# A sorted-block attention and its feed-forward layer on one core: loads issued ahead of GpSimd's own work, and every engine's list ordered anew

## The chip, the cores and the metric

The kernel runs on one core of a Trainium2 chip. A core has five engines that run side by side, each with its own list of instructions, taken strictly in order: TensorE (PE, matrix products; its loads of weights are shown as PEld), VectorE (DVE), ScalarE (ACT), GpSimd (POOL) and SyncE (SP). They wait for one another on semaphores. Transfers are issued from an engine's list (here from GpSimd and SyncE) and then run by themselves. The metric is device time in microseconds (us); less is better.

## What is computed

Four batches of eight heads, 768 positions, head size 64. Eight blocks of 96 keys and values per head are mixed by an 8x8 matrix P, which five rounds of a Sinkhorn iteration make from `sort_net`; then each block of queries attends to its own mixed block, and the result goes through a feed-forward layer of 2048 with a learned slope for negative values.

```python
P = sort_net                                   # [4, 8, 8, 8]
for _ in range(5):
    P = np.exp(P - max over the last axis)
    P = P / sum over the last axis
    P = P / sum over the axis before it
k_sorted = einsum('bhij,bhjcd->bhicd', P, k in blocks)     # v the same
attn = softmax(q_b @ k_sorted_b.T / 8)                     # per block of 96
x = (attn @ v_sorted_b), heads side by side                # [3072, 512]
h = x @ w_in                                               # [3072, 2048]
out = (max(h, 0) + alpha * min(h, 0)) @ w_out              # [3072, 512], float32
```

## The kernel before

The kernel is written as a graph. Each call of `G.add` names an engine (or a choice of engines), a function that issues the instructions, the keys that it reads and writes, a duration for a plan, and for a transfer its semaphore. There are 1222 such operations, numbered in the order in which they are added. The order in which they run is a table, `SEQ`: a list of these numbers. Each engine's list is the part of the table that belongs to it; a letter after a number (`97a`, `91d`) chooses ScalarE, VectorE or GpSimd where there is a choice.

`arrange` walks through the table and gives each operation a planned start and end, from durations and delays that are written in the code. The plan issues nothing by itself. It is used in two places: `emit` works out from the graph which semaphore waits are needed, and `fill` and `idle` put filling products into TensorE's list where the plan shows it waiting. These (line 1054) multiply the identity by itself into a free accumulator bank. `fill` works from the end of the bfloat16 identity `identb`, 5 us at the earliest, up to the second attention product; in a gap it puts 0.9 times the gap over 0.215 us of them.

The work of the opening, by the lines of the profile. Copies between tiles go through one helper and are all shown at line 429.

- Line 949: `BURST`, 110 products of 32x32 on zeros, at the start of TensorE's list.
- Lines 480, 464, 955, 963: loads from GpSimd, which convert to bfloat16: v and k of batch 0 (`VST`, `KS`), q (four parts), two halves of `w_in`, two of `w_out`. All go through one GpSimd queue.
- Lines 507, 521, 535: GpSimd's memsets. Line 507 clears `VDz`, the tile into which v is copied; for batch 0 in two halves, key `VD0`. Line 512: the select that makes the identity.
- Lines 579 to 593: the Sinkhorn steps on VectorE, with the exponential on ScalarE (582). Their result is `Pb`. Lines 600 and 604 spread it to the mixing matrix `BDK`.
- Line 657: the products that mix k of batch 0 (six steps), copied to `KT`; line 745: the same for v (eight steps), copied to `VS`, from `VDz`, whose eight pieces were copied from `VST` before (`conv_v`, line 723 of the file).
- Lines 782, 788, 794, 803, 826, 835: the attention of a head group (one block of all eight heads of a batch; 32 groups in all): score products, maximum, scores again with the maximum subtracted, exponential, product with v. Groups 0 to 7 take this path. Groups from 8 on use lines 782, 788, 815 (eight exponentials), 820 (a transposing transfer) and 835.
- Lines 884, 894, 897: FFN1, a step of four products, with ScalarE making `t` and VectorE making `hT`. Line 923: FFN2, a step of four products.

For batches 1 to 3, v's copies go into a ring of four slots of `VDz` (`conv_v`, second part), 64 partitions at a time: the lower half on GpSimd, the upper half too, but for batch 1 on ScalarE or VectorE as the table says.

## Time and profile before

| what | us |
|---|---|
| median of three timed runs | 248.17 |
| lowest, highest of them | 247.64, 251.79 |
| the profiled execution, its own time | 245.73 |
| its span in the trace | 243.7 |
| first FFN1 product starts | 28.98 |
| first FFN2 product starts | 40.83 |
| first score product of group 8 starts | 61.31 |

A row of the timeline gives the start, the busy time, the engine, the line and the operation, what it writes and reads (partitions x elements), how many instructions are merged, and in brackets how long the engine stood idle before it and what ended that. A busy TensorE is not TensorE at its peak: products are pipelined and their ends are modelled.

### The profile page before, as it was taken

Reading aid. Unit: us, or ns where it says so; the run is one execution under the profiler, and the core shown is the slowest. Engines: PE = TensorE matmul, PEld = TensorE weight load, DVE = VectorE, ACT = ScalarE, POOL = GpSimd, SP = SyncE. Lnnn points to the kernel's source line nnn. Section 1 sums busy time; section 2 is a strip of 40 time slices with the busy share of each in tenths; the row PEclk is TensorE's granted clock in tenths of the full one; section 3 lists DMA queues with packets and bytes.
Section 4 is the critical chain, followed back from the end, with each engine's and each line's share of the span. In section 5 each row is a group of like instructions: output and inputs, shape, how many; then the busy total and the mean of one; then the engine's idle time right before and its main releaser. Section 6 shows DMA issues by size and latency. Waiting matters only on the chain.

```text
span 243.7 us, 6078 instructions
## 1 busy us (share of the span) xinstructions
PE 224.3 (92%) x2410; PEld 135.5 (56%) x2439; DVE 174.6 (72%) x346; ACT 153.6 (63%) x422; POOL 101.4 (42%) x143
## 2 busy tenths in 40 slices
PE   1099999999877999999999999999999999999995
PEld 1056677886533666665655566555555555555553
DVE  5655589896999997878877787867777766554440
ACT  4327756767777799776885876667745674454331
POOL 7628282739799984528494954100000000000000
PEclk9999999999999999999999999999999999999999
DMA  5998999987999836762999443542453225312113
GB/s 95 197 200 124 190 208 210 172 154 107 215 152 106 76 97 127 168 133 42 172 148 175 119 56 70 120 113 54 90 158 66 52 75 67 102 39 92 42 46 129
DMA packets 65213, 28.99 MB, mean 119 GB/s; under 512 B 56849, under 2 KB 59937, under 8 KB 65185
## 3 DMA queue, kind: packets, MB, share of 16 engines
q0 software_dynamic: 25856, 13.64, 42.0%
q1 hardware_dynamic: 39328, 14.97, 28.8%
q8 instruction: 19, 0.31, 0.5%
q14 instruction: 10, 0.07, 0.1%
HBM read 27.28 MB, written 6.29 MB: 138 GB/s over the span
## 4 chain that ended last, share of the span: by engine, by line
PE 81%; DVE 9%; DMA 3%; ACT 3%; issue 2%; ACTq 0%; POOLq 0%
PE psH L884 30%; PE psYP L923 27%; PE psS L923 4%; PE psS L782 3%; DMA VST<-in_v_dram 3%; PE psO L835 3%; DVE VDz L429 3%; PE psYP L1054 3%; DVE hT L897 2%; PE psYP L699 2%; PE psYP L740 2%; PE psS L794 1%; PE psYP L884 1%; DVE VS L429 1%; PE psO L860 1%
## 5 line engine op out<-in xcount | busy, mean ns | idle before, releaser
L897 DVE SCALAR_TENSOR_TENSOR hT<-t,omaT,psH 128x384 bf16<-128x384 f32 (+1 forms) x131 | 74.9, 580 | 32.8 <-ACT t L894 31.5
L884 PE MATMUL psH<-xT,w_in_bf 128*128 128x384 bf16 (+1 forms) x524 | 95.2, 315 | 1.2 <-DVE hT L897 1.1
L894 ACT ACTIVATE t<-psH 128x384 f32<-128x384 f32 (+1 forms) x131 | 61.1, 470 | 50.4 <-PE psH L884 45.7
L923 PE MATMUL psYP<-w_out_bf,hT 128*128 128x512 bf16 x308 | 78.1, 379 | 1.7 <-issue 0.3
L884 PEld LDWEIGHTS psH<-xT,w_in_bf 128*128 128x128 bf16 x524 | 46.6, 98 | 31.1 <-DVE hT L897 3.4
L815 ACT ACTIVATE Esb<-psS,nf 96x96 bf16<-96x96 f32 x192 | 46.2, 344 | 2.5 <-DVE nf L788 2.4
L923 PEld LDWEIGHTS psYP<-w_out_bf,hT 128*128 128x128 bf16 x336 | 30.6, 98 | 28.8
L429 POOL COPY VDz<-VST 64x384 bf16<-64x384 bf16 (+1 forms) x45 | 38.1, 847 | 14.1 <-DMA VST<-in_v_dram 6.6
L686 POOL COPY KSz<-KS 64x512 bf16<-64x512 bf16 x36 | 22.0, 612 | 22.7 <-PE psYP L699 15.1
L788 DVE TENSOR_REDUCE nf<-psS 96x8 f32<-96x768 f32 x24 | 22.8, 949 | 4.8 <-PE psS L782 4.7
L455 POOL DMA_DIRECT2D QN<-in_q_dram x24 | 19.9, 845 | 9.0 <-PE psO L674 5.4
L845 DVE TENSOR_TENSOR xq<-psO,rec 96x512 bf16<-96x512 f32 x31 | 21.2, 685 | 0.8
L1054 PE MATMUL psYP<-identb 128*128 128x512 bf16 x21 | 7.6, 464 | 9.8 <-ACT identb L429 9.8
L835 PEld LDWEIGHTS psO<-VS,ET 112*128 112x128 bf16 x248 | 11.1, 97 | 3.9 <-ACT xT L429 0.2
L835 PE MATMUL psO<-VS,ET 112*128 112x65 bf16 x248 | 12.7, 194 | 0.0
L782 PE MATMUL psS<-KT,QT 64*96 64x96 bf16 x248 | 11.7, 214 | 0.1
L782 PEld LDWEIGHTS psS<-KT,QT 64*96 64x96 bf16 x248 | 7.9, 120 | 6.9 <-ACT t L894 2.2
L740 PEld LDWEIGHTS psYP<-BDV,VDz 128*128 128x128 bf16 x192 | 7.9, 98 | 6.7 <-DVE VDz L429 2.1
L740 PE MATMUL psYP<-BDV,VDz 128*128 128x64 bf16 x192 | 9.6, 193 | 2.2 <-DVE VDz L429 1.2
L429 ACT ACTIVATE outstg<-psYP 128x512 f32<-128x512 f32 x15 | 9.1, 604 | 3.8 <-PE psYP L923 3.7
L842 DVE RECIPROCAL rec<-psO 96x8 f32<-96x8 f32 x31 | 6.2, 200 | 6.6 <-PE psO L835 6.4
L429 ACT ACTIVATE VS<-psYP 112x512 bf16<-112x512 f32 x14 | 9.6, 686 | 2.0 <-PE psYP L740 1.8
(129 smaller groups left out, 206.9 us busy)
## 6 DMA issues: line engine op xcount, KB each, us to landing
out_dram<-outstg SPq DMA_DIRECT2D x23, 256.0 KB, 2.4
QN<-in_q_dram POOLq DMA_DIRECT2D x26, 96.0 KB, 4.3
KS<-in_k_dram POOLq DMA_DIRECT2D x3, 768.0 KB, 10.7
w_in_bf<-in_moe_w_in_dram POOLq DMA_DIRECT2D x2, 1024.0 KB, 11.6
w_out_bf<-in_moe_w_out_dram POOLq DMA_DIRECT2D x2, 1024.0 KB, 16.0
VST<-in_v_dram POOLq DMA_DIRECT2D x4, 384.0 KB, 6.4
VST<-in_v_dram POOLq DMA_DIRECT2D x1, 768.0 KB, 7.5
VST<-in_v_dram POOLq DMA_DIRECT2D x4, 192.0 KB, 4.5
```

Of the source, the lines that this page charges most:

```text
L429: return e.activation(o, i, ACTF.Copy) if e is nc.scalar else e.tensor_copy(o, i)
L686: G.add(POOL, lambda e, hp=hp: e.tensor_copy(AP(KSz, hp * 64 * 3072 + u % 3 * 1024 + hp * 64, [[3072, 64], [128, 8], [1, 64]]), AP(KS[n], ...
L740: inst = e.matmul(AP(t, off + dd * 64, [[row, 128], [1, 64]]), AP(VDz, (u % VSL * 8 + dd) * 128, [[VSL * 1024, 128], [1, 128]]), AP(BDV, b ...
L782: inst = e.matmul(o, AP(QT[n], hp * 64 * 3072 + h4 * 768 + i * 96, [[3072, 64], [1, 96]]), AP(KT[n], hp * 64 * ld + (i * 4 + h4) * bk, [[l ...
L788: G.add(DVE, lambda e: e.tensor_reduce(AP(nx, 0, [[8, 96], [4, 2], [1, 4]]), AP(psX, 0, [[1024, 96], [512, 2], [96, 4], [1, 96]]), AxisLis ...
L815: inst = e.activation(AP(Esb[me], p * 128, [[1024, 96], [64, 2], [1, 48]]), AP(psX, (p // 4) * 512 + (p % 4) * 96, [[1024, 96], [48, 2], [ ...
L835: inst = e.matmul(AP(psZ, hp * 512 + h4 * 68, [[1024, 128], [1, 65]]), AP(ET[me] if far else ET[m], pos(h4, hp) * 96, [[800, nk], [1, 128] ...
L845: G.add(DVE, lambda e: e.tensor_tensor(out=AP(xq[me], 0, [[512, 96], [256, 2], [64, 4], [1, 64]]), in0=AP(psZ, 0, [[1024, 96], [512, 2], [ ...
L884: inst = e.matmul(AP(pt, poff, [[1024, 128], [1, n]]), AP(w_in_bf, kt * DFF + ft * 128, [[KT_TILES * DFF, 128], [1, 128]]), AP(xT, kt * XR ...
L894: G.add(ACT, lambda e: e.activation(AP(t1[tb], 0, [[384, 128], [1, n]]), AP(pt, poff, [[1024, 128], [1, n]]), ACTF.Relu, scale=-1.0), t_ac ...
L897: G.add(DVE, lambda e: e.scalar_tensor_tensor(out=AP(hT, ft * RING + tok % RING, [[FT_TILES * RING, 128], [1, n]]), in0=AP(t1[tb], 0, [[38 ...
L923: inst = e.matmul(AP(bank[0], bank[1], [[1024, 128], [1, n]]), AP(hT, ft * RING + tok % RING, [[FT_TILES * RING, 128], [1, 128]]), AP(w_ou ...
```

## The change

- `SEQ` is a new order of all operations, and some choices of engine in it differ. One operation is gone (the two memsets of `VD0` are one), so the numbers from 20 on stand for the operation after.
- In GpSimd's list the identity's select comes right after v's load, then k, all four parts of q, both halves of `w_in` and the first half of `w_out`, then the memset of `VD0` and three copies of v. Before, memsets and copies stood between these loads, and the second half of `w_in` and both of `w_out` came after five copies of v.
- Copies of v of batch 0: from five on GpSimd, one on ScalarE, two on VectorE to three, one and four. On ScalarE and VectorE they stand behind the last Sinkhorn step of that engine.
- `identb` is ScalarE's first operation; it was behind the fifth exponential.
- `VD0` clears only the pad columns 48 to 63 of each 64 of `VDz`, in one memset of 128x512 in strips of 8, and not all of it.
- `BURST` is 226.
- Over the whole program ScalarE takes four copies of v of batch 1 (one before) and VectorE four (seven before); 15 copies of KT (12) fall to ScalarE, 11 of xT (7) to VectorE.
- Constants of the plan change: the engines' first free times, the delay after a block of TensorE instructions (6000 to 5500 ns), three durations. `behind` is recorded with an operation; no line shown here reads it.

```diff
-BURST = 110
+BURST = 226
 SEQ = """
-4 18 5 2 3 14 0 15 40 41 42 26 43 44 45 46 27 47 48 49 50 37 19 51 52 53 54 55 30 56 57 58 59 60 61 62 97a 6 7
+2 4 21 14 18 15 17 16 3 0 39 40 41 42 43 44 45 46 47 25 48 49 36 50 51 5 52 53 54 37 55 56 57 58 59 6 7 8 60
...
-    def add(self, eng, fn, dur, r=(), w=(), prio=0.0, dma=None, modes=(0, 0), how="load"):
+    def add(self, eng, fn, dur, r=(), w=(), prio=0.0, dma=None, modes=(0, 0), how="load", behind=()):
         op = _Op(eng, fn, dur, prio, dma, len(self.ops))
-        op.modes, op.how = modes, how
+        op.modes, op.how, op.behind = modes, how, [x.idx for x in behind]
...
-        free = {"pool": 400.0, "sync": 0.0, "pe": 0.0, "act": 1200.0, "dve": 0.0}
+        free = {"pool": 1300.0, "sync": 800.0, "pe": 1040.0, "act": 2050.0, "dve": 870.0}
...
-                    usable = y + (3300 if y < 3000 else 6000 if y < 38000 else 4500 if y < 66000 else 2600)
+                    usable = y + (3300 if y < 3000 else 5500 if y < 38000 else 4500 if y < 66000 else 2600)
...
-        zero_v("VD0", -95.5, [])
+        G.add(POOL, lambda e: e.memset(AP(zv, 24, [[VSL * 512, 128], [32, 64], [1, 8]]), 0.0), 640,
+              w=[("VD0", 0), ("VD0", 1)], prio=-95.5)
...
             G.add(EITHER if b == 1 and th else POOL, lambda e, o2=o2, i2=i2: copy(e, o2, i2),
-                  {"act": 868, "dve": 525, "pool": 835}, r=vst, w=[("VDz", u % VSL, th)], prio=prio)
+                  {"act": 868, "dve": 900, "pool": 845}, r=vst, w=[("VDz", u % VSL, th)], prio=prio)
```

## The prediction

> **What bounds the kernel now.** I read the page first: busy shares, slices, chain.

> ```profile
> PE 224.3 (92%) x2410; PEld 135.5 (56%) x2439; DVE 174.6 (72%) x346; ACT 153.6 (63%) x422; POOL 101.4 (42%) x143
> PE   1099999999877999999999999999999999999995
> PE 81%; DVE 9%; DMA 3%; ACT 3%; issue 2%; ACTq 0%; POOLq 0%
> ```

> TensorE is busy 92% of the span and makes 81% of the chain. The slices show two weak places: the first 12 us, and the slices from about 61 to 79 us. Then I asked for the busy time in stretches and, for the early part, the timeline.

> ```profile
> 18.00:23.00 5.00, 5.00 (x105) 2.96 (x100) 2.91 (x5) 3.79 (x7) 4.11 (x6) 1.00 0.78 107
> 61.31:79.25 17.94, 14.64 (x147) 7.69 (x149) 17.25 (x25) 13.76 (x40) 15.99 (x20) 1.00 1.22 158
> 82.00:240.00 158.00, 156.42 (x1302) 89.74 (x1324) 110.78 (x194) 101.67 (x293) 45.75 (x64) 1.00 0.52 96
> ```

> The columns are length, then busy time of PE, PEld, DVE, ACT, POOL, granted clock, DMA share and GB/s. From 82 us on TensorE misses 1.6 us of 158, so a new order of the lists can gain next to nothing there. From 61.31 to 79.25 it misses 3.3 us while VectorE is busy 17.25 of 17.94: VectorE is the bound of that stretch. So the gain has to come from the opening and from that stretch.

> **The change, part by part.** *Sinkhorn.* The chain of small VectorE and ScalarE steps that ends in Pb:

> ```profile
> 4.83 0.26 ACT L582 ACTIVATE P<-P 32x64 f32<-32x64 f32 x1 [1.31 <-DVE P L593]
> 6.59 0.26 ACT L582 ACTIVATE P<-P 32x64 f32<-32x64 f32 x1 [0.98 <-DVE P L593]
> 8.10 0.21 DVE L593 TENSOR_TENSOR P<-P,cs 32x64 f32<-32x64 f32 x1
> 8.93 0.85 ACT L429 ACTIVATE VDz<-VST 128x384 bf16<-128x384 bf16 x1 [2.09 <-DMA VST<-in_v_dram]
> 9.69 0.24 ACT L582 ACTIVATE P<-P 32x64 f32<-32x64 f32 x1
> 12.95 0.31 DVE L593 TENSOR_TENSOR Pb<-P,cs 32x64 bf16<-32x64 f32 x1
> ```

> An iteration takes 6.59 - 4.83 = 1.76 us. The fourth exponential should start at 6.59 + 1.76 = 8.35 and starts at 9.69, because ScalarE, in order, has a copy of v ahead of it that waits for v to land. The new list puts no copy of v on ScalarE before the fifth exponential, so Pb ends 1.34 us earlier: 13.26 becomes 11.92. The fill of sel0, ahead of the fourth reduction on VectorE, goes to before the first, where VectorE waits for sort_net.

> *From Pb to the first k product.*

> ```profile
> 1.04 1.07 PE L949 MATMUL psS<-bz 32*32 32x32 bf16 x110 [1.04 <-DVE bz L943]
> 11.95 1.89 PE L1054 MATMUL psYP<-identb 128*128 128x512 bf16 x4 [9.84 <-ACT identb L429]
> 13.77 0.38 PE L600 MATMUL psYP<-Pb,sel 32*128 32x8 bf16 x8
> 14.08 1.46 PE L1054 MATMUL psYP<-identb 128*128 128x512 bf16 x3
> 14.19 0.29 DVE L604 TENSOR_TENSOR BDK<-mkh,psYP 128x128 bf16<-128x128 f32 x1 [0.93 <-PE psYP L600]
> 15.94 0.69 PE L657 MATMUL psO<-BDK,KS 64*64 64x64 bf16 x32
> 21.35 1.25 PE L1054 MATMUL psYP<-identb 128*128 128x512 bf16 x5
> ```

> BDK is there at 14.48 and the k products start at 15.94: the filling products before them ran at 1.89/4 = 0.47 us each, at 21.35 the same five took 0.25 each. The filling is counted out in the plan at 0.215. The change makes identb before the first exponential (it was after the fifth), so the filling can run from about 5 us: (11.9 - 5.0) x 0.9 / 0.215 gives some 29 products, 25 if the plan puts the end of the 226 opening products near 5.9. The granted clock says 1.00 in every stretch, so the slow rate shows in durations alone. It lasted from 11.95 to 15.54, 3.6 us; 8 products go slowly, 17 to 21 at 0.215, 7.1 to 8.1 us in all, from 5.3 to 12.4 or 13.4. That overruns Pb by 0.5 to 1.5; before, the product L600 also stood 13.77 - 13.26 = 0.51 behind Pb. I keep 0.51, and BDK ends 1.22 after Pb as before, at 13.1, with TensorE fast; if nothing overruns, at 12.6.

> [...]

> The 226 cost TensorE 226 x 1.07/110 = 2.2 us that it otherwise idles; nothing waits for it before 5 us. A pause within them, bounded by Pb at 11.92, is hidden too.

> *Loads.*

> ```profile
> 2.66 0.29 POOL L512 TENSOR_SCALAR_AFFINE_SELECT identf<-identf 128x128 f32<-128x128 f32 x1
> 3.00 0.95 POOL L507 MEMSET VDz<- 128x1024 f32 x1
> KS<-in_k_dram POOLq DMA_DIRECT2D x1, 768.0 KB, 10.7
> 20.30 0.79 POOL L955 DMA_DIRECT2D w_in_bf<-in_moe_w_in_dram  x1
> 43.89 1.27 POOL L686 COPY KSz<-KS 64x512 bf16<-64x512 bf16 x2 [5.87 <-DMA KS<-in_k_dram]
> ```

> The select now stands before k's issue (0.3 us later, with v's bytes still ahead), after which seven issues follow with no fill between. k, issued at 1.98, lands at 12.7; so it is the next thing late, at 12.7 to 13.0, level with BDK. The second w_in, issued at 20.30 behind copies and fills, goes to about 7 (k's issue and five more ahead of it, at most 0.8 each). The stretch from 18 to 23 us moved 107 GB/s; filling that in ends the later loads about 2.5 us sooner, which GpSimd's 5.87 us wait at 43.89 feels and TensorE, busy there, does not. I cost it at nothing; the cover is that wait being GpSimd's own. One memset of 128x512 in strips replaces two of 128x1024: between 0.3 and 0.95 us, and under the loads either way.

> *The opening after BDK.* The new list gives VectorE, between BDK and the first attention product (L835), four copies of v, three of KT, four of VS, two maxima and six small pieces.

> ```profile
> L429 DVE COPY VDz<-VST 128x384 bf16<-128x384 bf16 x2 | 1.3, 640 | 0.0
> L429 DVE CAST KT<-psH 128x512 bf16<-128x512 f32 x3 | 2.0, 685 | 0.0
> L429 DVE CAST VS<-psO 112x512 bf16<-112x512 f32 x1 | 0.7, 693 | 0.7 <-PE psO L745 0.7
> L788 DVE TENSOR_REDUCE nm<-psS 96x8 bf16<-96x768 f32 x1 | 1.0, 955 | 2.1 <-PE psS L782 2.1
> 14.39 0.38 DVE L540 TENSOR_REDUCE mkjV<-identf 128x8 f32<-128x128 f32 x1
> 25.76 0.30 PEld L835 LDWEIGHTS psO<-VS,ET 112*128 112x128 bf16 x8
> ```

> The copies of v are 0.64 here and 0.99 from 61 to 79 us, where GpSimd copies beside them (next part). GpSimd's copies in the opening are listed first and end about 12, so I take 0.64; by 0.99 it is 1.4 us more and the gain below is 0.6.

> [...]

> The sum is 4 x 0.64 + 3 x 0.69 + 4 x 0.69 + 2 x 0.95 = 9.3, with 1.3 for the six (each at most 0.38) 10.6. From 13.1 this ends at 23.7, against 25.76 now: 2.0 us earlier. Bounds: Pb alone, less an overrun of 1, leaves 0.3; with BDK at 12.6 it is 2.5. Before, VectorE had idle time in this stretch (2.1 us ahead of the first maximum); now it is the bound.

> *The stretch of 61 to 79 us.* It runs from the first score product of head group 8 to its attention product. VectorE made seven copies of v here (the second halves), and ScalarE one; the new list gives four to each.

> ```profile
> L429 DVE COPY VDz<-VST 64x384 bf16<-64x384 bf16 x7 | 6.9, 987 | 0.2
> L894 ACT ACTIVATE t<-psH 128x384 f32<-128x384 f32 x8 | 4.0, 495 | 3.0 <-PE psH L884 3.0
> L429 ACT ACTIVATE VS<-psYP 112x512 bf16<-112x512 f32 x4 | 2.7, 687 | 0.8 <-PE psYP L740 0.8
> L429 ACT ACTIVATE VDz<-VST 64x384 bf16<-64x384 bf16 x1 | 0.9, 872 | 0.0
> 63.02 1.93 ACT L815 ACTIVATE Esb<-psS,nf 96x96 bf16<-96x96 f32 x8 [0.22 <-DVE nf L788]
> 117.25 1.30 PE psH L884 x8
> 121.60 1.73 PE psYP L923 x8
> ```

> VectorE's list there is now 4 maxima, 4 VS, 4 copies of v and 3 hT: 3.8 + 2.8 + 3.9 + 1.8 = 12.3. ScalarE becomes the bound: 3 x 1.93 + 4 x 0.50 + 4 x 0.87 + 4 x 0.69 + one out copy of 0.6 = 14.6, against 17.94: 3.3 us less. But the stretch now holds 4 FFN1 and 7 FFN2 steps where it held 7 and 6; 3 x 0.65 - 0.86 = 1.1 us of products moves to where TensorE is full. The net is 2.2. ScalarE's copies queue ahead of its exponentials; if each of its sixteen pieces waits 0.14, nothing remains; if the moved products fit into holes, 3.3.

> *The rest.* The planner's constants and the recorded `behind` issue no instruction; they reach the chip through the list and the filling counts. From 82 us on: nothing, plus or minus 1.

> **The sum.** 2.0 + 2.2 = 4.2 us off the profiled 245.73 (span 243.7 and 2 us around it): 241.5. The three timed runs have a median of 248.17, 2.4 above that execution; off it, the time is 244.0.

> **The rivals.** *More comes of it (241.5).* BDK ends at 12.6, the moved products fit, and the holes between 29 and 61 us shrink: 0.5 + 1.1 and 0.9 of the idle there:

> ```profile
> 28.00:32.00 4.00, 3.63 (x62) 2.51 (x62) 2.40 (x8) 2.53 (x6) 0.79 (x1) 1.00 1.17 177
> 45.00:60.00 15.00, 14.74 (x212) 11.53 (x213) 11.48 (x29) 11.03 (x27) 10.32 (x19) 1.00 1.13 139
> ```

> For it: k lands early enough, and v and k of the second batch come sooner. Against it: those 0.4 and 0.3 us of idle are mostly waits of one head group's own chain, which the change keeps.

> *ScalarE takes VectorE's place (246.2).* Its copies of v push the exponentials, and the middle gains nothing; 2.0 remains. For it: ScalarE was already 13.76 busy of 17.94. Against it: its list sums to less than the stretch.

> *The filling overruns (slower: 252.7 to 255.9).* If the array stays at the slow rate, 29 products of 0.47 take 13.6 us, from 5.3 to 18.9; L600, BDK and VectorE's 10.6 us follow and L835 comes at 19.6 + 10.6 = 30.2, 4.5 us late; from the plan's 5.9 it is 5.1. With the middle unchanged that gives 252.7 to 253.3, and it decides once more than 17 products run slowly. Against it: the rate changed 3.6 us after the filling began. For it: nothing in the list can skip a filling product. It goes past 254 if ScalarE's three more copies (2.6) also come on top in the middle.

> **How the numbers follow.** The forecast has 0.40, and its own range is 242.5 to 246; two fifths of it lie under 243.2, which is 2% off 248.17 (about what a measurement of this kernel can tell from no change). The rival with more has 0.30, ScalarE 0.12, the overrun 0.18, three fifths of it over 2%. Faster: 0.16 + 0.30 = 0.46; slower: 0.11; the rest, 0.43, within. The range from 240.5 to 250 takes in the first three cases and their bounds, and leaves out most of the overrun.

> **What would show it.** Right: the fourth exponential near 8.35, Pb near 11.9, the k products at 13 and the first L835 near 23.7; then a stretch from the first score product of group 8 to its L835 under 16 us, with ScalarE fuller than VectorE. Wrong: filling products still running when Pb is there by over 1 us, k products waiting for k's load, or a late L835 of group 8 with ScalarE idle.

## The result and the profile after

| what | before | after |
|---|---|---|
| median of four timed runs | 247.9 | 244.66 |
| lowest, highest of them | 247.26, 251.79 | 243.8, 248.17 |
| the profiled execution, its own time | 245.73 | 243.8 |
| its span in the trace | 243.7 | 242.0 |
| first k product | 15.94 | 14.03 |
| first attention product (the prediction's L835) | 25.76 | 26.40 |
| first FFN1 product | 28.98 | 30.22 |
| first score product of group 8 | 61.31 | 63.32 |
| attention product of group 8 | 79.25 | 76.88 |

Time after over time before is 0.9866, with a 95% interval of 0.9819 to 0.9913: the changed kernel is faster, by less than 2%. One execution of each kernel (251.79 and 248.17), over 1.5% longer than the fastest of its own, is left out of this ratio. The forecast was 244.0. That the number fits hides that one half of the sum went the other way: the opening, forecast 2.0 us shorter, became longer, and the rest of the program gained about what was forecast.

In the changed file the lines of the table of before stand one to three further down: L583 is the exponential, L587 and L594 the two-input Sinkhorn steps, L602 the spread of Pb, L606 BDK, L659 the k products, L747 the v products, L784, L790 and L817 the scores, maximum and exponentials, L837 the attention product, L886 and L925 FFN1 and FFN2, L951 the opening products, L1057 the filling.

Page of the kernel after: busy time, slices, granted clock in slices, chain.

```profile
PE 230.2 (95%) x2545; PEld 138.8 (57%) x2574; DVE 172.1 (71%) x350; ACT 152.3 (63%) x420; POOL 98.1 (41%) x140
PE   3997999999999999999999999999999999999995
PEclk9999799999999999999999999999999999999999
PE 83%; ACT 8%; DVE 4%; issue 3%
```

The weak slices at 61 to 79 us are gone, and the first three are fuller, since opening products and filling now stand there. New are a 7 of TensorE's in the fourth slice (18 to 24 us) and a 7 in the row of the granted clock, in the fifth; before, that row held nines only.

Timeline of the kernel after, the opening, all engines:

```profile
1.00 2.02 PE L951 MATMUL psS<-bz 32*32 32x32 bf16 x223 [1.00 <-DVE bz L945]
6.14 0.21 PE L951 MATMUL psS<-bz 32*32 32x32 bf16 x3 [3.12 <-issue]
6.28 6.99 PE L1057 MATMUL psYP<-identb 128*128 128x512 bf16 x24
8.29 0.26 ACT L583 ACTIVATE P<-P 32x64 f32<-32x64 f32 x1 [1.51 <-DVE P L594]
8.95 2.62 POOL L429 COPY VDz<-VST 128x384 bf16<-128x384 bf16 x3 [0.26 <-DMA VST<-in_v_dram]
9.04 0.81 DVE L587 TENSOR_TENSOR P<-P,rs 32x64 f32<-32x64 f32 x1
10.40 0.35 DVE L594 TENSOR_TENSOR P<-P,cs 32x64 f32<-32x64 f32 x1
12.30 0.21 DVE L594 TENSOR_TENSOR Pb<-P,cs 32x64 bf16<-32x64 f32 x1
13.20 0.37 PE L602 MATMUL psYP<-Pb,sel 32*128 32x8 bf16 x8
14.03 0.44 PE L659 MATMUL psH<-BDK,KS 64*64 64x64 bf16 x16
21.99 0.38 PE L747 MATMUL psO<-BDK,VDz 128*64 128x64 bf16 x11 [1.50 <-issue]
22.40 0.69 DVE L429 CAST VS<-psO 112x512 bf16<-112x512 f32 x1 [1.81 <-PE psO L747]
26.40 0.54 PE L837 MATMUL psO<-VS,ET 112*128 112x65 bf16 x8
```

Three things are to be seen. TensorE stops twice with "issue" as the reason: it waits for nothing that the trace shows. The first stop (3.12 us, three products short of the end of the 226) is hidden; the second (1.50, to 21.99) isn't: VectorE stands idle 1.81 us for its product. Then, the Sinkhorn step at 9.04 took 0.81, and the same step 0.21 in the other rounds; it began 0.09 after GpSimd's copies of v. And L602 starts at 13.20, 0.69 behind Pb (12.30 + 0.21), because the filling ends at 13.27.

Windows of the kernel after; behind the busy times stands the granted clock.

```profile
23.00:24.00 1.00, 1.00 (x37) 0.95 (x35) 1.00 (x5) 0.72 (x2) 0.00 (x0) 0.64 1.28 156
24.00:25.00 1.00, 1.00 (x10) 0.18 (x4) 0.82 (x3) 0.66 (x2) 0.00 (x0) 0.50 1.33 147
26.00:27.00 1.00, 1.00 (x16) 0.88 (x15) 0.02 (x1) 0.36 (x1) 0.00 (x0) 0.66 1.19 219
63.32:76.88 13.56, 12.75 (x140) 6.97 (x142) 10.36 (x16) 13.42 (x38) 11.22 (x14) 1.00 1.07 127
```

The trace's record of the clock has it halved from 23.28 to 26.69, 3.4 us, beginning 1.3 us behind the second stop; TensorE is "busy" throughout, at a granted clock of 0.50 (two filling products stand 0.41 apart in it, 0.22 behind it). By half of the 3.41 us that costs some 1.7, an estimate. The last row is the stretch of group 8: 13.56 us in place of 17.94, with ScalarE full (13.42) and VectorE at 10.36.

### The profile page after: what moved, and what is told of

It is laid out like the page before. It is cut to its first block, busy times and chain, and to the rows that moved or that the text cites. A ratio compares the mean times of both kernels' runs of the same rounds, so it can differ in the third digit from the quotient of the medians.

```text
span 242.0 us, 6334 instructions
## 1 busy us (share of the span) xinstructions
PE 230.2 (95%) x2545; PEld 138.8 (57%) x2574; DVE 172.1 (71%) x350; ACT 152.3 (63%) x420; POOL 98.1 (41%) x140
## 4 chain that ended last, share of the span: by engine, by line
PE 83%; ACT 8%; DVE 4%; issue 3%
PE psH L886 30%; PE psYP L925 27%; PE psYP L1057 4%; PE psS L925 4%; ACT Esb L817 3%; PE psO L837 3%; PE psS L784 3%; PE psYP L742 2%; PE psYP L701 1%; PE psS L796 1%; DVE hT L899 1%; ACT VDz L429 1%; ACT t L896 1%; PE psO L747 1%; ACT VS L429 1%
## 5 line engine op out<-in xcount | busy, mean ns | idle before, releaser
L886 PE MATMUL psH<-xT,w_in_bf 128*128 128x384 bf16 (+1 forms) x524 | 93.7, 315 | 0.2
L925 PE MATMUL psYP<-w_out_bf,hT 128*128 128x512 bf16 x309 | 78.5, 379 | 1.8 <-issue 0.5
L886 PEld LDWEIGHTS psH<-xT,w_in_bf 128*128 128x128 bf16 x524 | 47.0, 98 | 29.6 <-DVE hT L899 3.4
L817 ACT ACTIVATE Esb<-psS,nf 96x96 bf16<-96x96 f32 x192 | 46.3, 346 | 5.1 <-DVE nf L790 5.0
L925 PEld LDWEIGHTS psYP<-w_out_bf,hT 128*128 128x128 bf16 x336 | 30.3, 98 | 28.7 <-ACT outstg L429 0.2
L429 POOL COPY VDz<-VST 64x384 bf16<-64x384 bf16 (+1 forms) x43 | 36.4, 847 | 15.2 <-PE psYP L742 8.3
L790 DVE TENSOR_REDUCE nf<-psS 96x8 f32<-96x768 f32 x24 | 22.8, 951 | 12.4 <-PE psS L784 12.3
L455 POOL DMA_DIRECT2D QN<-in_q_dram x24 | 19.7, 846 | 13.4 <-PE psO L676 13.4
L847 DVE TENSOR_TENSOR xq<-psO,rec 96x512 bf16<-96x512 f32 x31 | 21.2, 685 | 0.8
L837 PEld LDWEIGHTS psO<-VS,ET 112*128 112x128 bf16 x248 | 11.0, 98 | 4.6 <-DVE xT L429 0.7
L837 PE MATMUL psO<-VS,ET 112*128 112x65 bf16 x248 | 12.9, 195 | 0.2
L784 PEld LDWEIGHTS psS<-KT,QT 64*96 64x96 bf16 x248 | 7.9, 120 | 8.1 <-ACT Esb L817 2.1
L784 PE MATMUL psS<-KT,QT 64*96 64x96 bf16 x248 | 11.7, 213 | 0.5 <-ACT Esb L817 0.4
L1057 PE MATMUL psYP<-identb 128*128 128x512 bf16 x40 | 11.9, 441 | 0.0
L429 ACT ACTIVATE outstg<-psYP 128x512 f32<-128x512 f32 x14 | 8.4, 600 | 5.0 <-PE psYP L925 5.0
L429 ACT ACTIVATE VS<-psYP 112x512 bf16<-112x512 f32 x14 | 9.7, 695 | 1.2 <-PE psYP L747 0.9
L429 ACT ACTIVATE KT<-psYP 128x512 bf16<-128x512 f32 x13 | 7.7, 595 | 3.6 <-PE psYP L701 3.6
## 6 DMA issues: line engine op xcount, KB each, us to landing
KS<-in_k_dram POOLq DMA_DIRECT2D x3, 768.0 KB, 10.2
w_in_bf<-in_moe_w_in_dram POOLq DMA_DIRECT2D x2, 1024.0 KB, 21.2
VST<-in_v_dram POOLq DMA_DIRECT2D x1, 768.0 KB, 7.5
```

What stands on the lines that cost most here:

```text
L429: return e.activation(o, i, ACTF.Copy) if e is nc.scalar else e.tensor_copy(o, i)
L784: inst = e.matmul(o, AP(QT[n], hp * 64 * 3072 + h4 * 768 + i * 96, [[3072, 64], [1, 96]]), AP(KT[n], hp * 64 * ld + (i * 4 + h4) * bk, [[l ...
L790: G.add(DVE, lambda e: e.tensor_reduce(AP(nx, 0, [[8, 96], [4, 2], [1, 4]]), AP(psX, 0, [[1024, 96], [512, 2], [96, 4], [1, 96]]), AxisLis ...
L817: inst = e.activation(AP(Esb[me], p * 128, [[1024, 96], [64, 2], [1, 48]]), AP(psX, (p // 4) * 512 + (p % 4) * 96, [[1024, 96], [48, 2], [ ...
L837: inst = e.matmul(AP(psZ, hp * 512 + h4 * 68, [[1024, 128], [1, 65]]), AP(ET[me] if far else ET[m], pos(h4, hp) * 96, [[800, nk], [1, 128] ...
L886: inst = e.matmul(AP(pt, poff, [[1024, 128], [1, n]]), AP(w_in_bf, kt * DFF + ft * 128, [[KT_TILES * DFF, 128], [1, 128]]), AP(xT, kt * XR ...
```

## The experiments

All kernels are edits of the kernel before or after. Each was timed in rounds beside the kernel before on the same chip; the times of before differ a little from one set of runs to the next (247.9 to 248.7). The steps in the traces are collected here: where the products behind Pb were stopped (length, and where the stop ended), the mean granted clock of the profiled execution, the start of group 8's scores, and what is left from there to the end of the span.

| kernel | median | Pb ends | first k | stops behind Pb | clock | first L837 | group 8 | rest |
|---|---|---|---|---|---|---|---|---|
| before | 247.9 | 13.26 | 15.94 | none | 1.000 | 25.76 | 61.31 | 182.39 |
| after | 244.66 | 12.51 | 14.03 | 1.50, 21.99 | 0.992 | 26.40 | 63.32 | 178.68 |
| after, again | 243.99 | 12.31 | 14.42 | 2.30, 23.20 | 0.993 | 27.34 | 64.50 | 178.70 |
| 110 opening products | 247.39 | 12.34 | 13.68 | 0.80, 21.46; 1.04, 28.46 | 0.979 | 24.78 | 65.49 | 180.31 |
| 8 filling products | 242.39 | 12.41 | 13.31 | 1.64, 21.83 | 0.999 | 24.55 | 61.34 | 178.76 |
| the same, again | 244.36 | 12.43 | 13.77 | 1.42, 23.14 | 0.986 | 27.46 | 65.24 | 178.76 |
| 8 filling, 290 opening | 245.99 | 12.50 | 13.40 | 1.73, 19.60; 2.74, 27.65 | 0.979 | 24.68 | 68.41 | 178.79 |
| four loads later | 244.21 | 11.72 | 14.25 | 1.46, 22.21 | 0.992 | 26.64 | 63.71 | 178.79 |
| GpSimd's copies behind Pb | 245.47 | 11.79 | 14.37 | 1.55, 22.41 | 0.993 | 26.50 | 63.70 | 178.70 |
| 8 filling and copies behind Pb | 243.26 | 11.72 | 12.94 | 1.69, 21.72 | 0.993 | 25.44 | 62.46 | 178.74 |
| the same, again | 242.84 | 11.70 | 13.48 | 0.48, 22.30 | 1.000 | 25.01 | 61.81 | 178.69 |
| after, old shares of v's copies | 244.53 | 12.35 | 14.15 | 1.16, 21.77 | 1.000 | 24.90 | 61.69 | 180.51 |
| before, new shares | 251.5 | 13.28 | 15.74 | none | 0.986 | 25.57 | 61.10 | 188.10 |
| before, Sinkhorn freed | 248.67 | 12.02 | 15.20 | 1.15, 24.36; 2.17, 32.74 | 0.993 | 27.10 | 66.19 | 182.41 |

The last column is the first finding. Nine traces with the new list and shares have 178.7 us (178.68 to 178.79) left from group 8's first score product on, whatever happened earlier; what differs between them is how late that product is. So the program falls into two parts that can be judged apart. (The tenth, with 110 opening products, has 1.6 more: in it alone TensorE waits 1.28 us for a transposing transfer, at 133 us.)

**110 opening products.** The plan and with it the filling stay as they are; only fewer products are issued.

```diff
-        for x in range(BURST):
+        for x in range(BURST if isinstance(e, _Count) else 110):
```

> The changed kernel with 110 opening products issued in place of 226; every other instruction, the filling counts too, as in the changed kernel. Theory (supply): TensorE's instructions come in blocks of 256, and the block that is asked for at one block start arrives 4 to 6 us later, so 226 products only run into the stop at 3.02 to 6.14 us sooner. Then: no stop ahead of the filling, which ends near 10 us; L602 right behind Pb, 0.6 us earlier than 13.20; the stop near 20.5 stays within half a us of 1.5 us; the first FFN1 0.4 to 0.8 us earlier than 30.22. Rival (the 226 products fetch the later blocks in time): the stops between Pb and the first FFN1 grow by over 1 us and the first FFN1 comes after 30.7.

Median 247.39 (243.13 to 247.76): three of the four executions, the profiled one too, had a mean clock of 0.979, and the one at 1.000 took 243.13, less than any of the kernel after in its first set. What the median loses comes with the halved clock. Timeline of this kernel, TensorE:

```profile
12.40 0.38 PE L602 MATMUL psYP<-Pb,sel 32*128 32x8 bf16 x8 [2.88 <-DVE Pb L594]
21.46 0.57 PE L747 MATMUL psO<-BDK,VDz 128*64 128x64 bf16 x23 [0.80 <-issue]
28.46 0.24 PE L676 MATMUL psO<-identb,QN 128*64 128x128 bf16 x1 [1.04 <-issue]
```

The stop in the opening products is gone, the filling ends in time and L602 follows Pb at once. But TensorE now stands idle for 2.88 us, the clock is halved from 12.4 to 15.8 us (and again from 29.5 to 36.3), and behind Pb there are two stops in place of one. Neither forecast was met: the stop was not 1.5 us at 20.5, and the first FFN1 came at 29.94, 0.3 earlier than in the kernel after. The opening products don't only pass the time; they place the stops.

**8 filling products ahead of Pb in place of 24**, the first of them tied to the end of the third Sinkhorn round.

```diff
                 n = int((op.start - begin) * 0.9 / unit)
+                n = n if out[1:] else min(n, most)
...
-                    x.deps.add(first)
+                    x.deps.add(first if out[1:] else tie)
```

> The changed kernel with 8 filling products ahead of Pb in place of 24, held back until the third Sinkhorn round is done. Theory (the filling costs twice, by its overrun and by its 32 extra instructions): L602 within 0.15 us of Pb, the stop near 20.5 shorter than 1 us, the granted clock 1.00 up to 30 us, the first FFN1 near 28.3 (30.22 before), and the execution 1.5 to 2 us shorter. Rival (the half clock from 23.4 to 26.6 us has nothing to do with the stop, or 8 products leave the array slow): the granted clock still falls to 0.5 or the first k products take 0.8 us in place of 0.44, and the first FFN1 gains under 1 us.

Median 242.39 (241.39 to 244.11), ratio to before 0.9796 (0.971 to 0.9881). Timeline, TensorE:

```profile
12.47 0.37 PE L604 MATMUL psYP<-Pb,sel 32*128 32x8 bf16 x8 [0.99 <-DVE Pb L595]
13.31 0.44 PE L661 MATMUL psH<-BDK,KS 64*64 64x64 bf16 x16
21.83 0.30 PE L807 MATMUL psS<-QT,KT 64*112 64x96 bf16 x3 [1.64 <-issue]
```

The spread follows Pb, k starts 0.72 earlier than in the kernel after. The stop did not get shorter, against what was expected: it moved on in the list, from the v products (L747) to the scores behind them (L807), and ended at the same time. The clock wasn't halved, and the first L837 came at 24.55. Whether that was the edit or luck needed a second look (below).

**The shares of v's copies, put into the kernel before, and taken out of the kernel after.** The order of each list is left; only five operations change engine.

```diff
+    for i, e in ((351, "act"), (353, "act"), (382, "act"), (390, "act"), (370, "dve")):
+        op = G.ops[i]
+        G.order[op.eng].remove(op)
+        op.eng = e
+        G.order[e].append(op)
+        G.order[e].sort(key=lambda o: o.start)
...
```

> The kernel before, with the batch-1 copies of v shared out as in the changed kernel (VectorE 7 to 4, ScalarE 1 to 4), at their places in the planned order; TensorE's list untouched. Theory (VectorE's load was the bound of the stretch from the first score product of group 8 to its first L835): the stretch goes from 17.94 us to 16 or less, the execution 1.5 to 2 us shorter. Rival (the new order made the gain): the stretch changes by under 0.7 us.

> The changed kernel, with the batch-1 copies of v shared out as before (VectorE 4 to 7, ScalarE 4 to 1), TensorE's list untouched. Theory (VectorE's load): the stretch from the first score product of group 8 to its first L837 goes from 13.56 us to 15.5 or more, the execution 1.5 to 2 us longer. Rival (order): under 0.7 us.

Before with the new shares: 251.5 (249.34 to 252.2), ratio 1.014 (1.0033 to 1.0247). Its stretch took 17.74 against 17.94: nothing gained. After with the old shares: 244.53 (243.88 to 245.92), and its stretch took 15.29 against 13.56. Groups of these two stretches, before with the new shares first, and after with the old ones:

```profile
L429 DVE COPY VDz<-VST 64x384 bf16<-64x384 bf16 x4 | 4.1, 1032 | 0.1
```

```profile
L429 DVE COPY VDz<-VST 64x384 bf16<-64x384 bf16 x7 | 4.2, 616 | 0.2
```

In the new order seven copies cost VectorE what four cost it in the old one. So the stretch's gain is not the sharing alone: the order brings 17.94 down to 15.29, and only in that order the shares bring another 1.73. Before with the new shares loses its time at another place, behind the stretch (timeline, GpSimd and TensorE):

```profile
125.07 2.48 POOL L455 DMA_DIRECT2D QN<-in_q_dram  x3 [7.38 <-DMA QT<-QN]
132.32 0.61 PE L740 MATMUL psYP<-BDV,VDz 128*128 128x64 bf16 x8 [2.82 <-POOL VDz L429]
```

There GpSimd waits 7.38 us for a transposing transfer, and v's copies for batch 3 come too late for TensorE; behind that the clock is halved from 131.3 to 138.1 us, which by half of its 6.8 us is another 3.4 us lost, an estimate. The one execution at a mean clock of 1.000 took 249.34.

**Four loads later, and GpSimd's copies later.** The stop at 22 us could be a matter of transfers in the way of instructions. In one kernel both halves of `w_out`, the second of `w_in` and k of batch 1 are issued after the opening; in the other GpSimd's three copies of v of batch 0 wait for Pb.

```diff
-                  r=vst + [("VD0", u // 4)], w=[("VD", u)], prio=prio, behind=[sorted_p])
+                  r=vst + [("VD0", u // 4)] + ["Pb"] * (u in (0, 1, 4)), w=[("VD", u)], prio=prio, behind=[sorted_p])
```

> The changed kernel with the second half of w_in, both halves of w_out and k of batch 1 issued behind GpSimd's pad copy of KT (near 17 us), about where the kernel before issued them; TensorE's list untouched. In the changed kernel and in two experiments the stop of TensorE in its v products or score products ended at 21.5 to 22.0 us, however many instructions stood before it. Theory (the transfers ahead of it hold the instruction block back): with the queues empty near 18 us, as before (107 GB/s), the block comes sooner, the stop near 20.5 shrinks from 1.5 to under 0.7 us, and the first FFN1 comes 1 to 2.5 us earlier than 30.22 (more if the half clock goes too). Rival (the block takes its 6 us anyway): the stop stays at 1.2 us or more and ends within 0.4 us of 21.9; the first FFN1 moves only with the clock.

> The changed kernel with GpSimd's three copies of v of batch 0 held back until Pb is there (they ran from 8.95 to 11.57 us beside Sinkhorn), and the last two loads issued ahead of them. Theory (a VectorE step with two inputs from the on-chip memory is held up while GpSimd copies: L587 took 0.81 us at 9.04 and 0.21 elsewhere, L594 0.35): Pb ends at 11.9 to 12.0 in place of 12.51. L602 follows only as far as the filling lets it (13.27), so the first FFN1 moves by under 0.4 us; VectorE's own copies of v get slower beside GpSimd's. Rival (the 0.81 has another cause): Pb stays at 12.3 or later.

Medians 244.21 (242.39 to 245.39) and 245.47 (244.15 to 247.55). The stop stayed in both (1.46 and 1.55): it is not these four transfers. With GpSimd's copies behind Pb the slow Sinkhorn step is gone and Pb ends at 11.79, where the prediction had it (11.92). That helped nothing, since the filling held L602 until 13.54. With the loads late, Pb ended at 11.72 although the copies ran beside the Sinkhorn steps from 8.96 on: there the step L586 had begun at 8.94, ahead of the copy (the part on the prediction comes back to this).

**Sinkhorn freed in the kernel before.** ScalarE's copy of v goes behind the fifth exponential; nothing else moves.

> The kernel before, with the one copy of v that stood ahead of ScalarE's fourth exponential put behind the fifth. Its plan puts 1 and 5 filling products around L600 in place of 4 and 3. Theory (the copy cost Sinkhorn 1.34 us): Pb ends near 11.9 in place of 13.26 and L600 starts within 0.6 us of it. How much of that reaches the first L835 (25.76): 0.8 to 1.4 us if VectorE and ScalarE set the opening; under 0.5 us if TensorE's instruction blocks set it, with a stop that is longer than the 0.42 us before.

Median 248.67 against 248.74, ratio 1.0032 (0.9991 to 1.0074). Timeline, TensorE:

```profile
12.38 2.31 PE L1053 MATMUL psYP<-identb 128*128 128x512 bf16 x5
...
17.31 0.70 PE L744 MATMUL psO<-BDK,VDz 128*64 128x64 bf16 x32
...
24.36 0.46 PE L793 MATMUL psS<-identb,nm 96*112 96x96 bf16 x5 [1.15 <-issue]
32.74 0.42 PE L883 MATMUL psH<-xT,w_in_bf 128*128 128x192 bf16 x3 [2.17 <-issue]
```

Pb came 1.24 earlier and k 0.74, but the five filling products behind Pb and then k's own ran at the slow rate, and by 17.31 this kernel was where before was at 17.32. An earlier Pb by itself is worth nothing in this list. That the first attention product came 1.3 later is not the edit's doing: both traces reach the scores' second product group at 22.86 and 22.87, and here TensorE stops in it, there it doesn't.

**Where the stops are.** Counted in the single records of TensorE's products and weight loads, each stop of over 0.45 us with "issue" as its reason has near one of four numbers of instructions ahead of it:

```
447         every kernel with 226 or 290 opening products
696, 698    before with Sinkhorn freed; 110 opening products
946 to 955  twelve traces
1209        290 opening products
```

They are some 256 apart: 250, 257 and 255 between 447, 697, 954 and 1209. What scatters the third by nine is not shown. In before the second of these places, count 697, is reached too, at 23.0, and nothing stops. The next run was made to test that: 64 more opening products, 128 instructions, on the kernel with 8 filling products.

> As e_fill8, but 290 opening products are issued in place of 226: 64 more, that is 128 more instructions of TensorE ahead of everything else, some 0.6 us of work at a time when TensorE waits anyway. Theory of the blocks of 256 instructions: the stops stay at counts near 448 and 960, and so the second one comes 128 instructions earlier in the list, among v's products that ran at 17.4 in e_fill8, and ends 6 to 7 us after count 704 was passed (near 14.3), at 20.5 to 21.2: a stop of about 3 us, first FFN1 near 29 and a further stop near count 1216 at 27 to 28; median 243 to 245.5. Rival (something ends at 21.5 to 22.4 whatever stands in the list): the stop ends at 21.5 to 22.4, just ahead of or within the same products (L747, L807) as before, 1 to 1.7 us long, and FFN1 starts near 28.3.

Median 245.99 (244.86 to 248.87), ratio 0.9922 (0.988 to 0.9965). Timeline, TensorE:

```profile
5.87 0.71 PE L953 MATMUL psS<-bz 32*32 32x32 bf16 x67 [2.85 <-issue]
17.53 0.34 PE L749 MATMUL psO<-BDK,VDz 128*64 128x64 bf16 x9
19.60 0.29 PE L749 MATMUL psO<-BDK,VDz 128*64 128x64 bf16 x7 [1.73 <-issue]
27.65 0.34 PE L839 MATMUL psO<-VS,ET 112*128 112x65 bf16 x6 [2.74 <-issue]
```

The theory of blocks of 256 instructions holds for the place: the stop came to the products forecast, those of 17.4 us, at a count of 955, and a new one appeared at 1209. The times were missed: it ended at 19.60 (forecast 20.5 to 21.2) and lasted 1.73 (forecast some 3), and the median is above the forecast 243 to 245.5. That most other stops had ended between 21.5 and 22.4 was a coincidence of similar lists.

The traces also hold what comes late. The pages count a queue named "instruction" (before, after, 290 opening products):

```profile
q8 instruction: 19, 0.31, 0.5%
```

```profile
q8 instruction: 20, 0.33, 0.6%
```

```profile
q8 instruction: 21, 0.34, 0.6%
```

Each of its transfers moves 16,384 bytes, and there is about one for every 256 of TensorE's records, of which these traces have 4849, 5119 and 5215 (255, 256 and 248 to a transfer). In the kernel after the first three ran from 2.61 to 4.65, from 9.83 to 10.72 and from 18.70 to 20.32; its stops ended at 6.14 and 21.99. Over all traces, each of the 25 stops ended 0.9 to 2.6 us behind the end of such a transfer, and of the 15 stops behind Pb all but two ended 1.3 to 1.7 behind it. In the opening each transfer but the first began 1.2 to 6.0 us after TensorE had come to the count before. From these places and times I take the stop to be TensorE waiting for its next block of instructions, the transfer of which in these traces began only after the block ahead of it had been begun; that is an inference, for the record of the stop says "issue" and no more.

Where one stop's end is followed by the next stop, the block's first instruction was there 7.0 us (110 opening products: 21.46 to 28.46), 8.1 (here: 19.60 to 27.65) and 8.4 us (before, Sinkhorn freed: 24.36 to 32.74) after the block ahead of it had been begun. The delay is not fixed, and before stood at its edge: its transfer ended at 20.72 and TensorE came to count 697 at 23.0, in time; with Sinkhorn freed the same transfer ended at 22.87, TensorE stood still from 23.21, and the stop was 1.15. Why a transfer begins sooner in one execution than in another is open. Between the one stop and the next TensorE used up its 256 instructions in 5.96, 5.31 and 6.21 us, sooner than the next were there. In the kernel after it went from count 698, at 15.45, to the stop at 20.49 in 5.04. From 55 us on 256 instructions took 11.1 us or more in before and after, and behind 40 us no trace shows such a stop.

**A second look at the 8 filling products, alone and with GpSimd's copies behind Pb; the kernel after once more.**

> The kernel after with 8 filling products ahead of Pb instead of 24, once more, in five rounds. If its gain over the kernel after is real (242.39 against 244.66 before), the median lies again between 241.5 and 243.5 and the ratio to the kernel before stays near 0.98; if it was luck with the half-clock window, the median lies near 244.5. Theory of the blocks: TensorE's stop shows at the same place of its list (behind about 957 instructions, the first products of L807) and ends at 21.8. Rival (the stop hangs on what the transfers do at that moment): its place or its length differ by over 0.5 us.

> As e_fill8, and GpSimd's three copies of v of batch 0 wait for Pb. [...] Theory of the blocks: the stop at count 957 still ends 6 to 7 us after count 704 is passed, so its end comes forward with k by about 0.5, to 21.2 to 21.5, and FFN1 to about 27.7; median 241.8 to 242.4. Rival (a fixed time): the stop still ends at 21.5 to 22.4 and the whole gives nothing: FFN1 at 28.2 and a median of 242.4 or, as v's late copies then cost VectorE or TensorE, 0.3 to 0.8 above it.

> The kernel after once more, unchanged, as the measure for the kernel with both edits in the same job. Theory (a stop of TensorE near 1.5 us lets the clock halve for some 3.3 us in most executions): stop at count 957 ending near 22, executions mostly at a mean clock of 0.986 to 0.993, median 244 to 245. Rival (the halved clock of the first executions was chance and goes away): most executions at clock 1.000, median 242.5 to 243.3.

> 8 filling products and GpSimd's copies of v behind Pb, once more, in five rounds beside the kernel after. Theory (the opening is shorter by 0.8 to 2.0 us because the filling no longer overruns Pb and Pb itself ends at 11.5): median 242 to 243.5, 1 to 2 us under the kernel after of this job. Rival (what is gained before the stop is given back in it and in the halved clock): median within 0.5 us of the kernel after.

The 8 filling products alone came to 244.36 (242.3 to 245.72), ratio 0.9825 (0.9775 to 0.9875): what was expected of luck, not of a gain. The stop was at the same place (954, the scores of L807) but ended 1.3 later, and the clock was halved from 23.5 to 30.3 us. With the copies behind Pb as well, 243.26 and 242.84, ratios 0.9795 (0.9741 to 0.985) and 0.9791 (0.974 to 0.9841). The first of these misses its forecast of 241.8 to 242.4: k came at 12.94, 0.37 ahead of the 8 alone (13.31), the end of the stop did not come forward with it (21.72), and the clock was halved behind it. The 8 products have a price of their own, which the rival of the first run had named: in two of the four traces with 8 filling and 226 opening products (the 8 alone again, and the second with the copies) the array was still slow when k came. Its first products took 0.63 in place of 0.44, and the full rate came at 16.7 and 17.3 us. Beside it in the same set the kernel after had 243.99, ratio 0.9852 (0.9797 to 0.9906). Six executions each, 241.68 to 243.49 against 243.08 to 246.28, and the medians 1.15 us apart: it is the fastest kernel of the study, though the intervals of the two ratios overlap. Its trace, VectorE (second set):

```profile
8.97 0.21 DVE L587 TENSOR_TENSOR P<-P,rs 32x64 f32<-32x64 f32 x1
11.49 0.21 DVE L594 TENSOR_TENSOR Pb<-P,cs 32x64 bf16<-32x64 f32 x1
```

The step that took 0.81 beside the copies takes 0.21 at the same time without them. k is then next: in that trace its first product waits 0.37 us for k's load, at 13.48.

## Why the prediction was right in the time and wrong in a half of its sum

Cut at the first attention product and at the stretch of group 8, the profiled executions compare so:

| part | forecast | measured |
|---|---|---|
| up to the first attention product | -2.0 | +0.64 |
| the stretch of group 8 | -3.3 | -4.38 |
| products moved out of it, before and after | +1.1 | +1.37 and +0.67 |
| sum | -4.2 | -1.70 |

**Sinkhorn: the freed exponential was right, Pb was not.** The fourth exponential starts at 8.29, forecast 8.35. Pb ends at 12.51, not 11.92. The prediction put GpSimd's copies to end "about 12" and asked what they do to VectorE's copies, which come later; it didn't ask what they do to VectorE's Sinkhorn steps, which run beside them. The step at 9.04, which has two inputs, lasted 0.81, against 0.21 in the other rounds, and ended at 9.85, 0.08 behind the end of the first of the three copies. That GpSimd's copies are needed for it is shown (without them 0.21, in three runs). What decides it is the moment at which the step starts, and the single records of the traces show it: 20 of these two-input steps, in eleven traces, began inside a copy of GpSimd with more than 0.13 us of it left, and every one ended 0.07 to 0.09 behind the end of that copy. The chain's reductions and reciprocals, which read one input, kept their 0.19 to 0.26 inside copies. In the kernel with late loads the step had begun 0.02 ahead of the copy, and the two steps that began inside one met only its last 0.15 and 0.16.

**The filling: the bound was right, the term too small.** The filling ended at 13.27, within the 12.4 to 13.4 that the prediction gave, but the sum kept only 0.51 us between a Pb at 11.92 and the spread. The spread (now L602) started at 13.20, 1.28 behind that, and BDK ended at 13.89, not 13.1. The late Pb was not to blame: with Pb at 11.79 (GpSimd's copies behind Pb) the spread started at 13.54. The rival, an array that stays slow for all 29 products, didn't come: the slow rate lasted 3.4 us from 6.28 and then ended. The prediction took the granted clock to be 1.00 while the products were slow. The record of the clock has no entry there: its first one stands at 15.76 in before and at 9.62 in after, about where the slow products end (15.54 and 9.65), and a view shows 1.00 where there is none.

**The step that failed is "now it is the bound", said of VectorE from BDK to the first attention product.** VectorE (third busy time of the window) was busy for 8.84 of the 12.51 us from BDK's end to 26.40, where 10.6 without a gap had been forecast:

```profile
13.89:26.40 12.51, 10.98 (x295) 7.95 (x295) 8.84 (x20) 6.38 (x12) 2.07 (x2) 0.88 1.22 172
```

TensorE stopped at 20.49, with "issue" as the reason, and VectorE waited for it. The prediction saw that opening products might pause and called a pause within them hidden. It was, 3.12 us of it. What it didn't follow is that 116 more opening products and 19 more filling products ahead of k move every later instruction 270 places along, and that the stops are tied to places. In before, TensorE came to count 697 at 23.0, 2.3 us behind the end of a transfer (20.72), and went on; now count 954 falls into the v products, with a stop of 1.5 us, and in most executions the halved clock comes behind it. Take the late k (0.9), the stop (1.5) and the halved clock (some 1.6, half of the 3.12 us that it lasts up to there) off 26.40, and 22.4 is left, or somewhat more where VectorE's own list would then have ended last; the forecast was 23.7. That is an estimate: no kernel with the new list was free of stops. In the trace with the old shares, with a stop of 1.16 and the clock full, that product came at 24.90.

**The middle: right mechanism, two terms mis-sized, against each other.** ScalarE did become the bound (13.42 of 13.56), and its sum of 14.6 was about 1 too long; its groups of instructions add up to 15.0 there as well, where it was busy for 13.42, since neighbouring instructions overlap. The copies, which cost VectorE 0.99 each before, cost 0.53 (groups of the kernel after, stretch):

```profile
L429 DVE COPY VDz<-VST 64x384 bf16<-64x384 bf16 x4 | 2.0, 530 | 0.1
L429 ACT ACTIVATE VDz<-VST 64x384 bf16<-64x384 bf16 x4 | 3.4, 862 | 0.1
```

The windows of before under one of its copies, and of after under three, show the difference; the fifth busy time is GpSimd's.

```profile
69.40:70.52 1.12, 1.10 (x12) 0.57 (x12) 1.11 (x1) 0.74 (x2) 1.12 (x2) 1.00 1.61 96
```

```profile
65.86:66.84 0.98, 0.98 (x15) 0.66 (x14) 0.98 (x2) 0.98 (x6) 0.04 (x1) 1.00 0.42 81
69.30:69.85 0.55, 0.55 (x8) 0.26 (x5) 0.55 (x1) 0.55 (x4) 0.44 (x2) 1.00 0.07 7
```

The single records tell why. All seven of before began inside a copy or a transfer issue of GpSimd's and ended 0.34 to 0.40 us behind its end. In after two began with GpSimd idle; the other two began in the last 0.15 us of a copy and of an issue (at 69.30, with the copy's end at 69.45, and at 71.24, with the issue's at 71.36) and ended 0.40 and 0.39 behind. So the price is not 0.99 wherever GpSimd copies beside VectorE, as the prediction took it to be, but the wait for what GpSimd is doing when the copy starts, and the order of the lists sets it.

The prediction saw that products move out of the stretch, and set a part of their price off. They cost it in full (windows of before, then of after, on both sides of the stretch; the first busy time is TensorE's):

```profile
25.76:61.31 35.55, 34.69 (x500) 26.13 (x504) 28.85 (x72) 23.50 (x57) 19.52 (x31) 1.00 1.23 171
79.25:243.70 164.45, 160.05 (x1346) 92.25 (x1367) 113.50 (x199) 104.41 (x303) 48.25 (x68) 1.00 0.52 97
```

```profile
26.40:63.32 36.92, 35.84 (x507) 26.56 (x509) 31.26 (x76) 22.98 (x56) 21.05 (x33) 1.00 1.33 178
76.88:242.00 165.12, 160.88 (x1350) 92.31 (x1371) 112.75 (x201) 105.07 (x305) 52.36 (x73) 1.00 0.58 100
```

TensorE's busy time fell by 1.89 in the stretch (14.64 to 12.75) and rose by 1.15 and 0.83 outside it: the same work elsewhere. What a stretch sheds to stretches that are full is not a gain. Net, the two terms give -2.34 where -2.2 was forecast.

**The time.** By the profiled pair the kernel gained 1.9 us where 4.2 was forecast; the medians differ by 3.2. The forecast carried over the 2.4 us by which before's profiled execution lay under its median; after's lay 0.9 under its own. That much of the good fit is the scatter of single executions.

**The rivals.** "More comes of it" fell (it needed BDK at 12.6 and free holes). "ScalarE takes VectorE's place" was half true: it took the place, and the middle gained all the same. The overrun was there, 0.8 us beyond the 0.51 allowed for, and far from the 18.9 us of that rival. The stop for instructions, which decided the opening, was none of them.

## What to carry to other kernels

Work added to an idle engine's list is not free because nobody waits for it: here it shifted every instruction behind it 270 places against the counts at which TensorE stopped (447, 697, 954, 1209), so count instructions as well as microseconds where products are as short as in this opening. Check a bound by asking of each engine whether it could run out of instructions or clock, not only of work. And judge a reordering by cutting the trace at points that both kernels share: here one cut separated an opening that scatters by 7 us from a rest that repeats within 0.1.
